# Giving out norm scalings two per step and moving three left-hand sums to other steps, in attention followed by a SwiGLU block

## The chip, the cores and the metric

The kernel runs on one core of a Trainium2 chip. A core has five engines that matter here, each with its own queue of instructions in program order: TensorE (PE, matmuls, with its weight loads shown as PEld), VectorE (DVE), ScalarE (ACT), GpSimd (POOL), and SyncE (SP), which issues the DMAs. The metric is the device time of one execution in microseconds (us); less is better. All arithmetic is in fp32.

## The reference: what is computed

Attention over 8 sequences, 12 heads, 448 positions and 64 dimensions a head, with queries and keys normalised by their root mean square, then a feed-forward block on the same rows.

```python
q_n, k_n = rmsnorm(q, g_q), rmsnorm(k, g_k)
attn = softmax(q_n @ k_n.T / sqrt(64))          # per sequence and head
x = (attn @ v)                                  # (8, 12, 448, 64) -> (3584, 768)
xn = x / sqrt(mean(x * x) + 1e-6) * rms_g
out = (silu(xn @ w_gate) * (xn @ w_val)) @ w_out   # 768 -> 1536 -> 768
```

## The kernel before

**Tiling and stages.** A loop runs over 48 pairs of heads (six to a sequence). The attention of a pair takes four PE steps of score and value matmuls. Between the pairs lie the feed-forward items of earlier sequences, some to each slot. When sequence s is through attention, its rows x are normalised by `norm_x` (L732). Then come the output products of sequence s-1, and after them the gate and value products of sequence s. The gate and value products (L1182) use a fast scheme of 15 block products for 3 by 3 blocks. The left operands that this scheme needs are sums of blocks of x, made on DVE by L772.

**The output product.** For sequences 2, 3, 5, 6 and 7 there are four tiles of 128 rows (some carried over from the sequence before), and `out_quads` (L1462) multiplies them with `w_out` by two nested levels of a seven-product scheme in Strassen's manner. The outer level has seven products, i = 0 to 6. The outer left sums are made by L1364. Inside each outer product i stand seven inner products, whose left operands are A11, A12, A22 and the four inner sums S1 = A21 + A22, S2 = S1 - A11, S3 = A11 - A21 (which is written over A21), S4 = A12 - S2. All inner sums are made on DVE by `left_q1` (L1384), so they all stand in the trace under L1392, and all are 128x384. An inner product is three matmuls in the program and six in the trace (an fp32 matmul shows as two records).

An outer product is done in four PE steps. Step `a` (12 records) uses A11 and A12, `bb` (12) S2 and then S3, `c` (12) A22 and then S1, `d` (6) S4. The order is a(0), bb(0), c(0), a(1), d(0), bb(1), c(1), a(2), d(1), and so on: **d(i) comes after a(i+1), and bb(i+1) comes right after d(i)**. At the very end c(6) is followed by d(6): in sequence 7 directly, in the others with one gate product between.

**What DVE does in each step.** After a(i), L1538 adds the two halves of a PSUM bank. After bb(i), L1543 and L1544 add into a running tile. After c(i), L1552 adds that tile to the bank of c. The matmuls of d(i) go into half of that same bank, so they can't begin before L1552 has read it. After d(i), L1564 adds the last piece, and `finish(i)` has POOL add whole tiles (L1489). Before the change, the sums are put there as follows, behind the adds of the same step in DVE's queue:

- bb(i): S4 of i, then S1 of i+1 (for i = 1, S1 comes in c instead)
- c(i): S2 and S3 of i+1 (for i = 1: first all outer sums still waiting, by `hurry`, then S1, S2, S3)
- d(i): none

Other DVE work falls between these steps: after each one, either one waiting outer sum (L1364) or one sum of x (L772) is issued, and DVE's reductions for the query and key norms (L496) come too.

**norm_x.** It puts a transposed 1/rms into a PSUM bank `rb` (from the four banks that the attention scores also rotate through), and six DVE instructions (L744, 128x448, for hp = 0 to 5) scale the six parts of x with it. The bank comes free after the sixth. For sequences 2 to 7, scaling hp is put behind the step hp steps later; for sequence 1 they go three per step, for sequence 0 all at once.

**What sets the order.** Nothing is planned by cost: `pe(fn)` counts one step, emits its instructions, and then those that `after(n, fn)` put off to this step. Every engine runs its queue in exactly that order.

Of the kernel before, what the change touches and what calls it, by code (L numbers as in the profile page):

```python
# [335 lines left out]
def safe_scores(  # L336
# [42 lines left out]
    def after(n, fn):  # L379
        due.append((now["t"] + n, fn))  # L380
# [351 lines left out]
    def norm_x(b):  # L732


        rs = st.pop(("rx", b))
        ps = (ps_s if b else ps_f).tile([128, 512], F32, name="rb", tag="s" if b else "f")
        for t in range(NT):
            nc.tensor.transpose(ps[:, t * P:(t + 1) * P], rs[:, t:t + 1].to_broadcast([P, 128]), ident[0:P, 0:P])

        whole = st["x", b]  # L740

        def scale(hp):
            x = whole[:, hp, :]
            nc.vector.scalar_tensor_tensor(x, x, rg[:, hp:hp + 1], ps[:, 0:S], ALU.mult, ALU.mult)  # L744

        for hp in range(NPAIR):
            if b:
                after(hp // 3 if b == 1 else hp, lambda hp=hp: scale(hp))
            else:
                scale(hp)  # L750
        if b == 0:
            return

        parts = st.pop(("x", b)).rearrange("p (h c) n -> p h c n", h=2)
        a = st["left", b] = {f"a{i + 1}{k + 1}": parts[:, :, k, i * HT:(i + 1) * HT] for i in range(2) for k in range(3)}

        def place(name):
            if name in OVER:
                return a[OVER[name]]
            if name in MADE[:4]:  # L760
                t = s_pool.tile([128, S], F32, name="xs")
            elif name in ("S2", "S0"):
                t = l2_pool.tile([128, S], F32, name="l2")
            else:
                t = more_x[("S4", "S5", "S13").index(name)]
            return t.rearrange("p (h n) -> p h n", h=2)

        def op(name):
            first, second, what = LEFT_G[name]
            one, two = a[first], a[second]  # L770
            a[name] = place(name)
            nc.vector.tensor_tensor(a[name], one, two, what)  # L772

        slow.extend((name, lambda name=name: op(name)) for name in MADE)
        st["x_at"] = now["t"]
# [46 lines left out]
    ORDER_Q = ("B11", "B21", "T2", "T3", "T4", "T1", "B22")  # L822
# [64 lines left out]
    def data(key):  # L887
        return st[key][0][:, 0:GW if key[0] == "wg" else BW]
# [99 lines left out]
    def out_pairs(b):  # L988
        return (((0, 1),), ((-1, 0), (1, 2)), ((-1, 0), (1, 2)), ((0, 1), (2, 3)))[b % 4]
# [394 lines left out]
    def left_q1(b, i, which):  # L1384

        of = lambda name: left_q(b, i, name)
        for at in which:
            to, first, second, what = (("S1", "A21", "A22", ALU.add), ("S2", "S1", "A11", ALU.subtract),
                                       ("S3", "A11", "A21", ALU.subtract), ("S4", "A12", "S2", ALU.subtract))[at]
            if to != "S3":  # L1390
                st["l2", b, i, to] = l2_pool.tile([128, S], F32, name="l2")[:, 0:KG * 128].rearrange("p (c n) -> p c n", c=KG)
            nc.vector.tensor_tensor(of(to), of(first), of(second), what)  # L1392
# [69 lines left out]
    def out_quads(b):  # L1462

        bank, dst, steps = {}, {}, []
        tiles = [i for pair in out_pairs(b) for i in pair]
        left = {}
        for key in stream_q(b):
            left[key] = min(2, PARTS_Q - 2 * key[3])

        def rows(name):  # L1470

            if name in ("B11", "T1"):
                tag = "pa"
            elif name in ("T2", "T3"):
                tag = {"T2": "pb", "T3": "pc"}[name]
            else:
                tag = None
            if tag:
                t = tmp.tile([128, 2, S], F32, name=tag, tag=tag, bufs=1)
                return [t[:, row, 0:BW] for row in range(2)]  # L1480
            return [y_pool.tile([128, HALF], F32, name="y", tag="y") for _ in range(2)]

        def out(what, n, first):
            for row in range(2):
                after(4, lambda row=row: store(b, n, tiles[first + row], what[row]))

        def add(to, one, other):
            for row in range(2):
                nc.gpsimd.tensor_tensor(to[row], one[row], other[row], ALU.add)  # L1489

        def finish(i):
            name, m = ORDER_Q[i], dst[i]
            if name == "B21":
                add(m, m, dst[0])
                out(m, 0, 0)
            elif name == "T2":
                add(m, m, dst[0])
            elif name == "T3":
                add(m, m, dst[2])
            elif name == "T4":  # L1500
                add(m, m, dst[3])
                out(m, 0, 2)
            elif name == "T1":
                add(dst[3], dst[3], m)
                add(m, m, dst[2])
                out(dst[3], 1, 2)
            elif name == "B22":
                for row in range(2):
                    nc.vector.tensor_tensor(m[row], m[row], dst[5][row], ALU.add)
                out(m, 1, 0)  # L1510

        def term(i, at, ps, start=True):

            a = left_q(b, i, ("A11", "A12", "S2", "S3", "A22", "S1", "S4")[at])
            for j in range(KG):
                n = at * KG + j
                key = ("wq", b, i, n // 2)
                nc.tensor.matmul(ps, lhsT=a[:, j, :], rhs=data(key)[:, n % 2 * HW:(n % 2 + 1) * HW], start=start and j == 0,  # L1518
                                 stop=j == KG - 1, skip_group_check=True)
                left[key] -= 1  # L1520
                if not left[key]:
                    used(key)

        def two(i, what):
            ps = bank[i, what] = ps_f.tile([128, 512], F32, name="ff", tag="f")[:, 0:BW].rearrange("p (h n) -> p h n", h=2)
            for h in range(2):
                term(i, 2 * "abc".index(what) + h, ps[:, h], start=h == 0)
            return ps

        def lo_hi(tile):  # L1530
            return tile[:, 0:HW], tile[:, HW:BW]

        def a(i):
            ps = two(i, "a")
            dst[i] = rows(ORDER_Q[i])
            q1 = st["q1", b, i] = tmp.tile([128, S], F32, name="th", tag="th", bufs=2)[:, 0:HW]
            nc.scalar.copy(q1, ps[:, 0])
            nc.vector.tensor_tensor(lo_hi(dst[i][0])[0], ps[:, 1], q1, ALU.add)  # L1538

        def bb(i):  # L1540
            ps = two(i, "b")
            u = st["u", b, i] = tmp.tile([128, S], F32, name="th", tag="th", bufs=2)[:, 0:BW].rearrange("p (h n) -> p h n", h=2)
            nc.vector.tensor_tensor(u[:, 0], ps[:, 0], st.pop(("q1", b, i)), ALU.add)  # L1543
            nc.vector.tensor_tensor(u[:, 1], ps[:, 1], u[:, 0], ALU.add)  # L1544
            left_q1(b, i, (3,))
            if i == 0 or i > 1 and i + 1 < len(ORDER_Q):
                left_q1(b, i + 1, (0,))

        def c(i):
            ps = two(i, "c")  # L1550
            u3 = st["u", b, i][:, 1:2].to_broadcast([128, 2, HW])
            nc.vector.tensor_tensor(dst[i][1].rearrange("p (h n) -> p h n", h=2), ps, u3, ALU.add)  # L1552
            if i == 1:
                hurry(first_sums)
                left_q1(b, i + 1, (0,))
            if i + 1 < len(ORDER_Q):
                left_q1(b, i + 1, (1, 2))
            if i + 2 == len(ORDER_Q):
                st["l2 done", b] = True

        def d(i):
            ps = bank[i, "c"]
            term(i, 6, ps[:, 1], start=False)
            nc.vector.tensor_tensor(lo_hi(dst[i][0])[1], ps[:, 1], st.pop(("u", b, i))[:, 0], ALU.add)  # L1564
            finish(i)

        full = 2 * KG * HW
        if b == B - 1:
            steps.append((0, idle))
        for i in range(len(ORDER_Q) + 1):  # L1570
            if i < len(ORDER_Q):
                steps.append((full, lambda i=i: a(i)))
            if i:
                steps.append((full // 2, lambda i=i - 1: d(i)))
            if i < len(ORDER_Q):
                steps += [(full, lambda i=i: bb(i)), (full, lambda i=i: c(i))]
        return steps
# [185 lines left out]
    scale = norm_rests(0, 0, 2)  # L1763
# [12 lines left out]
    for g in range(NG + 1):  # L1776
        b, hp = divmod(g, NPAIR)
# [138 lines left out]
```

## Time and profile before

| what | us |
|---|---|
| median of 3 runs (1531.54 to 1534.40) | 1532.55 |
| the execution that was profiled | 1533.21 |
| span of its instructions in the profile | 1531.4 |
| PE busy in that span | 1484.1 |
| DVE busy | 1039.9 |
| POOL busy | 738.6 |
| ACT busy | 604.0 |

The profiled execution is 1.8 us longer than its span, which is what lies around the first and last instruction. It is 0.66 us above the median. In the lines of the profile, "x<-a,b" names the tile written and the tiles read, L is the line of the kernel, and a bracket at the end gives the idle time of the engine before the instruction and what ended it. Times of the trace are counted from the start of the span. The output products of sequence 2 begin at 616.0, of sequence 3 at 804.7, of sequence 6 at 1330.8 and of sequence 7 at 1471.6. Sequence 5's repeat those of sequence 3 some 344 us later.

### The profile page before, as it was taken

The numbers are of one execution on the slowest core, as the hardware profiler recorded it, in microseconds if no ns is written. First come the engines' busy times: TensorE is split into PE (matmuls) and PEld (weight loads), VectorE is DVE, ScalarE is ACT, GpSimd is POOL, SyncE is SP. The second block draws the span as 40 slices with busy tenths as digits, with TensorE's granted clock in tenths as the row PEclk, the third lists the DMA queues.
The fourth block names the chain that finished last, engine by engine and source line by source line (L and its number), as shares of the span: only waits on it lengthen the run. The fifth ranks groups of instructions, "written<-read, shape, count | busy, mean of one in ns | idle before, by whom it ended". The sixth has DMA issues, their size and how long they took to land.

```text
span 1531.4 us, 25718 instructions
## 1 busy us (share of the span) xinstructions
PE 1484.1 (97%) x8732; PEld 1155.8 (75%) x8732; DVE 1039.9 (68%) x1826; ACT 604.0 (39%) x1377; POOL 738.6 (48%) x708
## 2 busy tenths in 40 slices
PE   8999999998999999899999999999999999999997
PEld 4344445687755888787988788759788789899996
DVE  5777999687855687874568655635668655674664
ACT  6856765344322443224442443334542443201100
POOL 6967987555433453364544644345644632021002
PEclk9999999999999999999999999999999999999998
DMA  7758675775577899885557865576457755597675
GB/s 190 224 164 237 183 237 169 231 250 187 188 235 231 283 309 317 285 254 191 174 152 237 247 186 160 162 228 190 133 162 246 223 157 145 154 301 227 167 237 170
DMA packets 302176, 322.51 MB, mean 211 GB/s; under 512 B 81620, under 2 KB 243668, under 8 KB 302036
## 3 DMA queue, kind: packets, MB, share of 16 engines
q1 hardware_dynamic: 301108, 320.58, 68.8%
q8 instruction: 72, 1.18, 0.3%
q14 instruction: 68, 0.56, 0.1%
q10 hardware_dynamic: 800, 0.20, 0.1%
q0 software_dynamic: 128, 0.00, 0.0%
HBM read 266.90 MB, written 53.77 MB: 209 GB/s over the span
## 4 chain that ended last, share of the span: by engine, by line
PE 83%; DVE 10%; DMA 2%; issue 2%; SPq 1%; ACT 1%; POOL 1%; DVEq 0%; POOLq 0%; ACTq 0%
PE ff L1182 37%; PE ff L1518 12%; PE sc L659 8%; PE av L674 7%; PE ff L1589 6%; PE ff L1447 5%; PE tr L545 2%; PE ff L1320 1%; PE den L692 1%; DVE l L1392 1%; PE den L607 1%; PE sc L563 1%; DMA vt<-in_v_dram 1%; PE av L590 1%; DVE ms L496 1%
## 5 line engine op out<-in xcount | busy, mean ns | idle before, releaser
L714 POOL TENSOR_TENSOR es<-es,e 128x448 f32<-128x448 f32 x205 | 252.2, 1230 | 13.6
L1182 PE MATMUL ff<-x,w 128*128 128x224 f32 x1272 | 254.0, 353 | 1.4 <-DVE pb L1203 1.1
L1182 PEld LDWEIGHTS ff<-x,w 128*128 128x128 f32 x1272 | 238.5, 190 | 4.2 <-DVE pb L1203 1.4
L659 PE MATMUL sc<-qT,kT 64*64 64x448 f32 x1176 | 232.7, 541 | 5.6 <-DVE x L744 3.9
L674 PE MATMUL av<-e,vt 64*64 64x448 f32 x984 | 193.3, 538 | 0.0
L664 ACT ACTIVATE e<-sc 128x448 f32<-128x448 f32 x294 | 155.0, 547 | 80.9 <-PE sc L659 59.4
L1182 PE MATMUL ff<-xs,w 128*128 128x224 f32 x848 | 168.4, 353 | 2.6 <-DVE w L1087 1.3
L1182 PEld LDWEIGHTS ff<-xs,w 128*128 128x128 f32 x848 | 158.6, 190 | 6.3 <-issue 3.4
L644 POOL TENSOR_TENSOR ss<-ss,rd 128x448 f32<-128x448 f32 x40 | 46.8, 1170 | 210.3 <-ACT rd L643 210.3
L659 PEld LDWEIGHTS sc<-qT,kT 64*64 64x64 f32 x1176 | 78.8, 133 | 88.2 <-issue 59.9
L709 POOL TENSOR_TENSOR es<-e 128x448 f32<-128x448 f32 x41 | 47.3, 1154 | 192.5 <-ACT e L664 192.5
L1518 PE MATMUL ff<-w,l 128*128 128x192 f32 x630 | 119.1, 331 | 6.8 <-DVE pb L1552 3.0
L1203 DVE TENSOR_TENSOR pc<-ff,l 128x448 f32<-128x448 f32 x56 | 34.9, 623 | 122.9 <-PE ff L1182 91.7
L515 POOL TENSOR_TENSOR rs<-ms,mhalf 128x12 f32<-128x12 f32 (+1 forms) x50 | 115.3, 2307 | 4.2
L1518 PEld LDWEIGHTS ff<-w,l 128*128 128x128 f32 x630 | 104.2, 191 | 13.8 <-DVE pb L1552 4.2
L1589 PE MATMUL ff<-x,w 128*128 128x448 f32 x288 | 111.8, 541 | 0.0
L674 PEld LDWEIGHTS av<-e,vt 64*64 64x64 f32 x984 | 66.0, 133 | 41.3 <-issue 41.3
L1200 DVE TENSOR_TENSOR pb<-ff,pb 128x448 f32<-128x448 f32 x84 | 52.4, 623 | 63.0 <-PE ff L1182 53.5
L1589 PEld LDWEIGHTS ff<-x,w 128*128 128x128 f32 x288 | 53.3, 190 | 51.1 <-issue 47.6
L1182 PE MATMUL ff<-top_x,w 128*128 128x224 f32 x424 | 89.4, 361 | 2.1 <-DVE w L1090 2.1
L1182 PEld LDWEIGHTS ff<-top_x,w 128*128 128x128 f32 x424 | 80.2, 193 | 13.4 <-issue 10.2
L1489 POOL TENSOR_TENSOR y<-y,pa 128x384 f32<-128x384 f32 x10 | 11.3, 1154 | 157.4 <-DVE y L1564 144.4
(210 smaller groups left out, 2892.2 us busy)
## 6 DMA issues: line engine op xcount, KB each, us to landing
w<-kept SPq DMA_DIRECT2D x383, 256.0 KB, 3.4
w<-kept_q SPq DMA_DIRECT2D x350, 192.0 KB, 3.8
w<-kept_o SPq DMA_DIRECT2D x150, 192.0 KB, 4.0
kept_q<-w SPq DMA_DIRECT2D x63, 192.0 KB, 3.4
qk<-in_q_dram SPq DMA_DIRECT2D x48, 192.0 KB, 3.8
qk<-in_k_dram SPq DMA_DIRECT2D x96, 96.0 KB, 3.8
raw<-in_moe_w_gate_dram SPq DMA_DIRECT2D x24, 384.0 KB, 4.5
raw<-in_moe_w_val_dram SPq DMA_DIRECT2D x24, 384.0 KB, 4.3
```

The source lines that it names most:

```text
L515: nc.gpsimd.tensor_tensor(st["rs", g][:, cols], ms, mhalf[:, cols], ALU.pow)
L644: after(m, lambda: (nc.gpsimd.tensor_tensor(ss, ss, rd, ALU.add), st.update({("summed", b): hp})))
L659: nc.tensor.matmul(ps[r, 0:S], lhsT=st["kT", g][r, keys_of(i)], rhs=st["qT", g][r, :], start=True, stop=True)
L664: nc.scalar.activation(e, ps[:, 0:S], ACT.Exp)
L674: nc.tensor.matmul(st["av", g][own(j), 0:S], lhsT=vt, rhs=st["e", g, i][r], start=i == 0, stop=i == PARTS - 1, skip_group_check=True)
L709: nc.gpsimd.tensor_tensor(st["es", g], st["e", g, 0], st["e", g, 1], ALU.add)
L714: nc.gpsimd.tensor_tensor(st["es", g], st["es", g], st["e", g, i], ALU.add)
L1182: nc.tensor.matmul(bank[:, w * HT:(w + 1) * HT], lhsT=data(key)[:, (2 * w + c) * 128:(2 * w + c + 1) * 128], rhs=a[left][:, c, :], start=o ...
L1200: nc.vector.tensor_tensor(T[name], ps[:, 0:S], T[name], ALU.add)
L1447: nc.tensor.matmul(ps, lhsT=left_o(b, which, LEFT_O[name], c), rhs=data(("wo", b, name, c)), start=first and c == 0, stop=c == NFP - 1, sk ...
L1518: nc.tensor.matmul(ps, lhsT=a[:, j, :], rhs=data(key)[:, n % 2 * HW:(n % 2 + 1) * HW], start=start and j == 0, stop=j == KG - 1, skip_grou ...
L1589: nc.tensor.matmul(bank[w][:, 0:S], lhsT=data(key)[:, c * 128:(c + 1) * 128], rhs=st["x", 0][:, 3 * half + c, :], start=half == c == 0, st ...
```

## The change

The scalings of `norm_x` for sequences 2 to 7 go two per step (steps 0, 0, 1, 1, 2, 2) instead of one (0 to 5). Of the inner sums, S4 of i moves from bb(i) to c(i), where it stands behind L1552 and ahead of everything else; S3 of i+1 moves from c(i) to d(i), behind L1564; S2 of i+1 stays in c(i), and now follows S4. No instruction is added or taken away, and no PE step moves.

```diff
         for hp in range(NPAIR):
             if b:
-                after(hp // 3 if b == 1 else hp, lambda hp=hp: scale(hp))
+                after(hp // (3 if b == 1 else 2), lambda hp=hp: scale(hp))
...
         def bb(i):
...
             nc.vector.tensor_tensor(u[:, 1], ps[:, 1], u[:, 0], ALU.add)
-            left_q1(b, i, (3,))
             if i == 0 or i > 1 and i + 1 < len(ORDER_Q):
                 left_q1(b, i + 1, (0,))
...
         def c(i):
...
             nc.vector.tensor_tensor(dst[i][1].rearrange("p (h n) -> p h n", h=2), ps, u3, ALU.add)
+            left_q1(b, i, (3,))
             if i == 1:
                 hurry(first_sums)
                 left_q1(b, i + 1, (0,))
             if i + 1 < len(ORDER_Q):
-                left_q1(b, i + 1, (1, 2))
+                left_q1(b, i + 1, (1,))
...
         def d(i):
...
             finish(i)
+            if i + 1 < len(ORDER_Q):
+                left_q1(b, i + 1, (2,))
```

In `left_q1` the numbers 0, 1, 2, 3 stand for S1, S2, S3, S4.

## The prediction

> **What bounds the kernel now.** I read the page first (busy shares), then the table of waits of TensorE, then the timeline of TensorE, VectorE and GpSimd through the output products of sequences 2, 3, 6 and 7.
>
> ```profile
> span 1531.4 us, 25718 instructions
> PE 1484.1 (97%) x8732; PEld 1155.8 (75%) x8732; DVE 1039.9 (68%) x1826; ACT 604.0 (39%) x1377; POOL 738.6 (48%) x708
> ```
>
> TensorE is busy for 97% of the span, so 1531.4 - 1484.1 = 47.3 us of idle time is all that a change of order can win. The waits of TensorE say which of it the moved instructions touch:
>
> ```profile
> PE sc L659 <- DVE x L744: 3.9, 1, 3.9
> PE ff L1518 <- DVE pb L1552: 3.0, 3, 1.0
> ...
> PE ff L1518 <- DVE pa L1552: 1.8, 4, 0.5
> ...
> PE ff L1518 <- DVE l L1392: 1.3, 2, 1.1
> ...
> PE ff L1518 <- DVE raw L1392: 0.5, 3, 0.2
> ```
>
> One score matmul waits for the last scaling (L744), since it takes over the bank rb. Steps d wait for L1552, steps bb for S2 (tile l) and S3 (raw). In these stretches VectorE is the late one: the end of sequence 3's output shows it without a gap.
>
> ```profile
> 861.24 0.54 DVE L1552 TENSOR_TENSOR pa<-ff,th 128x384 f32<-128x384 f32 x1
> 861.70 1.31 DVE L1392 TENSOR_TENSOR l<-l,raw 128x384 f32<-128x384 f32 x1
> 862.93 1.48 DVE L1392 TENSOR_TENSOR raw<-raw 128x384 f32<-128x384 f32 x1
> 864.34 0.61 DVE L772 TENSOR_TENSOR l<-x,top_x 128x448 f32<-128x448 f32 x1
> 864.87 0.34 DVE L1538 TENSOR_TENSOR y<-ff,th 128x192 f32<-128x192 f32 x1
> 865.14 0.61 DVE L772 TENSOR_TENSOR l<-x,top_x 128x448 f32<-128x448 f32 x1
> 865.67 0.34 DVE L1564 TENSOR_TENSOR pa<-ff,th 128x192 f32<-128x192 f32 x1
> ```
> ```profile
> 861.83 2.47 PE L1518 MATMUL ff<-w,l 128*128 128x192 f32 x12 [0.51 <-DVE pa L1552]
> 864.47 2.22 PE L1518 MATMUL ff<-w,raw 128*128 128x192 f32 x12 [0.16 <-DVE raw L1392]
> ```
> ```profile
> 858.52 5.48 POOL L714 TENSOR_TENSOR es<-es,e 128x448 f32<-128x448 f32 x4
> ```
>
> S2(6) and S3(6) take 1.31 and 1.48 instead of 0.55 us beside four GpSimd adds. S3(6) ends at 864.41, and TensorE goes on with bb(6)'s second half at 864.47. Where VectorE isn't behind, as in sequence 7, the rhythm is this:
>
> ```profile
> 1493.48 2.11 PE L1518 MATMUL ff<-w,l 128*128 128x192 f32 x12
> 1495.43 1.79 PE L1518 MATMUL ff<-w,h 128*128 128x192 f32 x10
> ```
> ```profile
> 1494.66 0.36 DVE L1564 TENSOR_TENSOR pb<-ff,th 128x192 f32<-128x192 f32 x1 [0.22 <-PE ff L1518]
> ```
>
> The first 12 records are d(2) and bb(3)'s S2 half, 0.975 us each. bb(3) begins at 1494.46, its S3 half at 1495.43, and L1564 starts 0.20 us after bb(3) began.
>
> [...] the sums measured alone take 0.55 us, and 1.3 to 1.5 us where L714 or L1489 runs; L1552, which has one input in PSUM, stays at 0.54. [...] After the 3.86 us gap the granted clock from 632 to 637 was 0.66, and score matmuls took 1.01 instead of 0.54 us.
>
> **Prices.** A VectorE instruction lets the next start after 0.27 us (128x192), 0.47 (a sum), 0.54 (L772) or 0.59 (L744); these are start-to-start distances. TensorE restarts 0.055 us after the end of the sum it waited for (1348.054 to 1348.109), and its next record then comes 0.267 instead of 0.163 us later. A wait therefore costs the end of the sum + 0.16 - the planned start.
>
> **Part 1, the scalings.** They are the same instructions, earlier. In sequence 2 the sixth started at 631.73, behind four sums L1150 to L1153 that GpSimd's adds stretched to 1.3 us; now it goes by 624. From the start of that attention block to bb(1)'s second half sequence 2 took 636.98 - 623.87 = 13.11 us, sequence 3, without the wait, 820.13 - 812.56 = 7.57. So 5.5 us can be won. Next late there is S3(1), see part 2. In the other sequences no wait on L744 over 0.1 us goes away. Against this, three steps carry 1.2 us more of VectorE each. In sequences 2 and 3 an attention block follows and hides it. In sequence 6 none follows: there VectorE is already late, L1552(0) starts at 1338.33 and d(0) starts 0.21 us late. Of the queue from 1331.32 on, the scalings hp 2 to 5 now stand ahead of L1552(0), where only hp 2 stood; S4(0) left. So L1552 moves by 3 x 0.59 - 0.47 = 1.3 to 1339.64, S4(0), now behind it, ends at 1340.66, and d(0), planned for 1338.57, is held for 2.25 instead of 0.47 us: **+1.8 us**.
>
> **Part 2, the sums.** Three things happen.
>
> *S3 comes just too late everywhere.* It now waits for d(i)'s matmuls and L1564. Counted from bb(i+1)'s start: L1564 at 0.20, S3 from 0.47 to 1.02, TensorE at 1.075; the S3 half was planned at 0.975. Cost 1.02 + 0.16 - 0.975 = 0.2 us for every clean transition. I count 2 clean ones each in sequences 2, 3, 5 and 6, and 4 in sequence 7. Only a turn of queries or keys between d and bb (0.33 to 0.43 us) hides it. In d(0) of sequences 3 and 5 a GpSimd add is running (the sum at 819.63 took 0.73): 0.4 us. [...] I take 0.2, because S3 starts before L1489.
>
> *S2(2) moves back by one sum in c(1)*, behind S4(1): it ended at 826.28, now 826.75, and bb(2) was due at 826.41: +0.5 us in sequences 2, 3, 5 and 7.
>
> *Where VectorE is behind, S3 now queues behind everything of steps c, a and d.* At i = 5 of sequence 3, S3(6) ended at 864.41. The four instructions that followed it, L772, L1538, L772, L1564, now stand ahead of it: 0.54 + 0.27 + 0.54 + 0.27 = 1.6 us, up to 2.0 with the lock at L772. bb(6)'s second half goes from 864.47 to 866.1 to 866.5; I take **+1.8 us** (range 1.0 to 2.2) for each of sequences 2, 3 and 5, with every wait before it absorbed. At i = 2, L1552(2) does come some 1.5 us earlier (S4(2) left its front, 0.66, and one lock), but d(2) needs S4(2), which is now 0.47 or, locked, 1.1 us behind L1552. Ends of S4(2) between 832.9 and 834.3 by who gets the lock, against a planned 832.3 to 832.8: the old wait of 1.26 becomes 0.8 to 1.7. I take no change. S3(3) then ends 0.27 us late.
>
> Sums by sequence. Sequence 3 (and 5): 0.4 + 0.5 + 0 + 0.3 + 0.2 + 1.8 (the second clean one is within the 1.8) + 0.1 for d(6) = 3.3 each. Sequence 2: after the attention block VectorE is busy with L1150 to L1153 until 631.8, so L1564(0) starts at 632.1, S3(1) ends at 632.9, and bb(1)'s second half goes from 636.98 to 632.96: -4.0, then + 0.5 + 0.3 + 0.2 + 1.8 + 0.1 = -1.1. Sequence 6: +1.8 for d(0); +0.5 for S3(1) behind L1538, an outer sum and L1564; -0.4 for S2(2), since VectorE catches up during the wait; +1.1 for S3(2) behind two L772; -0.4 for d(2); +0.4, +0.2, +0.2, +0.4 for S3(3) to S3(6); +0.2 for d(6): +4.0. Sequence 7: 0.4 + 0.5 + 4 x 0.2, and at the end d(6), which waits for L1552 anyway (0.71 us), now also for S4(6), which ends at 1520.06: +0.4, together +2.1. The S4 of the other steps has 1.95 us of a(i+1) as cover and needs 1.2; without a(i+1) it would cost what it costs at the end.
>
> Total: 3.3 + 3.3 - 1.1 + 4.0 + 2.1 = **+11.6 us** on the profiled 1533.21; on the median of the runs 1532.55 + 11.6 = 1544.2.
>
> **Rivals.** (a) *The wait sums are partly absorbed*: only the firm terms hold (12 clean S3 at 0.2 = 2.4, S2(2) 2.0, half of the i = 5 terms 2.7, half of sequence 6's d(0) 0.9, tail 0.4, less 4.0 in sequence 2): +4.4, 1537. For it: a stall gives VectorE time to catch up. Against it: S3's chain starts at TensorE itself. (b) *Gain and loss cancel*, within 0.2% (about 3 us, what a measurement here can tell from no change): 1532.5. It needs i = 5 to cost nothing. (c) *Faster*: the lightened bb decides. If S3 is in time, that is, if L1564 and S3 together take under 0.92 us after bb's start (I find 1.02) and VectorE has no queue at d, then all listed waits go: 5.5 in sequence 2, 2.7 in each of 2, 3 and 5 (1.26 at d(2), 1.46 from d(5) on), 2.2 in 6, 0.5 in 7 = 16.3; less the tail 0.4: 1516.6. For it: L1552 is the commonest releaser, and it does move forward. Against it: d then waits for S4 behind L1552, and the timeline above has a queue at d(5).
>
> **How the numbers follow.** Forecast (+7 to +18) 0.60, (a) 0.20, (b) 0.08, (c) 0.12. Slower 0.80, same 0.08, faster 0.12. Own range of the forecast: 1540 to 1550. With (a) and the edge of (b) the range is 1533 to 1550, leaving out (c) and the tails.
>
> **What would show it.** Right: weight loads of L1518 wait for `h L1392` and `raw L1392` at nearly every bb, and matmuls over 1 us at bb(6) of sequences 2, 3 and 5 (a clean wait of 0.1 us leaves no gap on the matmul row, whose records overlap by 0.16; it shows in their starts); `x L744` is gone; L1552 gives way to `l L1392` (S4) at d(2). The step d to bb's second half in sequence 7 goes from 1.95 to 2.15 us. Wrong: waits on L1392 no more than before, or bb(6) with no wait. The whole is wrong if the stretches of sequences 2 to 7 come out shorter.

## The result and the profile after

The changed kernel takes 1547.26 us (median of 6 runs, 1546.62 to 1549.11), against 1533.47 us for the kernel before in the same comparison: a ratio of 1.0091, 95% interval 1.0072 to 1.0111. It is slower by 13.8 us. The forecast was 1544.2, that is +11.6.

The page of the profile after, engines and span:

```profile
span 1544.8 us, 25720 instructions
PE 1489.5 (96%) x8732; PEld 1154.2 (75%) x8732; DVE 1044.1 (68%) x1826; ACT 603.9 (39%) x1377; POOL 742.9 (48%) x708
```

The span grew by 13.4 us. TensorE's idle time grew from 47.3 to 55.3 us, and its busy time by 5.4: the first record after a wait is itself longer (0.43 instead of 0.33 us), and the first 0.16 us of a wait lie under the record before it, where they count as busy. The work is the same, so order alone cost this. The table of TensorE's waits in the profile after (total us, times, longest):

```profile
PE ff L1518 <- DVE l L1392: 9.8, 17, 2.0
PE ff L1518 <- DVE raw L1392: 6.3, 5, 1.8
...
PE ff L1518 <- DVE h L1392: 3.2, 5, 1.3
```

The waits on L744 and on the add behind c (L1552, now L1551) have left the table. In their place stand 19.3 us of waits on inner sums: on `l`, which is S4 (and S2), and on `raw` and `h`, which is S3. Before, sums held TensorE for 1.8 us in all.

For each sequence I compared the stretch from the first to the last matmul of its output product. Times are us, relative to the kernel before:

| stretch of sequence | forecast | measured |
|---|---|---|
| 2 | -1.1 | -0.9 |
| 3 | +3.3 | +4.3 |
| 5 | +3.3 | +4.1 |
| 6 | +4.0 | +4.2 |
| 7 | +2.1 | +2.15 |
| sum | +11.6 | +13.9 |

These five stretches hold the whole loss; outside them the span shrank by 0.5 us. The clean rhythm of sequence 7, which the prediction showed for before, TensorE first, then VectorE:

```profile
1505.52 2.11 PE L1518 MATMUL ff<-w,l 128*128 128x192 f32 x12
1507.57 2.22 PE L1518 MATMUL ff<-w,h 128*128 128x192 f32 x12
```
```profile
1506.69 0.36 DVE L1564 TENSOR_TENSOR pb<-ff,th 128x192 f32<-128x192 f32 x1 [0.22 <-PE ff L1518]
1506.97 0.55 DVE L1392 TENSOR_TENSOR h<-h 128x384 f32<-128x384 f32 x1
```

d(2) to bb(3)'s second half now takes 2.05 us instead of 1.95, and the half itself 0.1 longer. S3 ends at 1507.52, TensorE starts at 1507.57. No idle time shows on the matmul row, since records overlap. The loss of 0.2 us shows only in the starts.

The end of sequence 3's output, which stood before the change at 861.24 to 865.67. VectorE, TensorE and GpSimd of the profile after:

```profile
861.16 1.31 DVE L1392 TENSOR_TENSOR l<-raw,l 128x384 f32<-128x384 f32 x1
862.40 1.48 DVE L1392 TENSOR_TENSOR l<-l,raw 128x384 f32<-128x384 f32 x1
863.80 1.55 DVE L772 TENSOR_TENSOR l<-x,top_x 128x448 f32<-128x448 f32 x1
865.28 0.34 DVE L1538 TENSOR_TENSOR y<-ff,th 128x192 f32<-128x192 f32 x1
865.54 0.61 DVE L772 TENSOR_TENSOR l<-x,top_x 128x448 f32<-128x448 f32 x1
866.08 0.34 DVE L1564 TENSOR_TENSOR pa<-ff,th 128x192 f32<-128x192 f32 x1
866.35 0.54 DVE L1392 TENSOR_TENSOR raw<-raw 128x384 f32<-128x384 f32 x1
```
```profile
862.53 1.24 PE L1518 MATMUL ff<-w,l 128*128 128x192 f32 x6 [0.37 <-DVE l L1392]
863.93 1.24 PE L1518 MATMUL ff<-w,l 128*128 128x192 f32 x6 [0.16 <-DVE l L1392]
866.94 2.22 PE L1518 MATMUL ff<-w,raw 128*128 128x192 f32 x12 [1.76 <-DVE raw L1392]
```
```profile
859.40 5.47 POOL L714 TENSOR_TENSOR es<-es,e 128x448 f32<-128x448 f32 x4
```

The rows are S4(5), S2(6), a sum of x, the add behind a(6), a sum of x, the add behind d(5), and only then S3(6). TensorE waits for that last row, 1.76 us. d(5) and the first half of bb(6) wait a little, as they did before, but d(5) now for S4(5) and no longer for the add of c.

### The profile page after: what moved, and what is told of

Its sections match the earlier page's. It is cut to its first block, busy times and chain, and to the rows that moved or that the text cites. A ratio compares the mean times of both kernels' runs of the same rounds, so it can differ in the third digit from the quotient of the medians.

```text
span 1544.8 us, 25720 instructions
## 1 busy us (share of the span) xinstructions
PE 1489.5 (96%) x8732; PEld 1154.2 (75%) x8732; DVE 1044.1 (68%) x1826; ACT 603.9 (39%) x1377; POOL 742.9 (48%) x708
## 4 chain that ended last, share of the span: by engine, by line
PE 80%; DVE 13%; DMA 2%; issue 1%; ACT 1%; POOL 1%; SPq 0%; DVEq 0%; POOLq 0%; ACTq 0%
PE ff L1182 37%; PE ff L1518 11%; PE sc L659 7%; PE av L674 7%; PE ff L1447 5%; PE ff L1591 5%; DVE l L1392 2%; PE tr L545 2%; PE ff L1320 2%; PE den L692 1%; PE sc L563 1%; PE den L607 1%; PE av L590 1%; DVE ms L496 1%; DVE xs L772 1%
## 5 line engine op out<-in xcount | busy, mean ns | idle before, releaser
L714 POOL TENSOR_TENSOR es<-es,e 128x448 f32<-128x448 f32 x205 | 251.2, 1225 | 13.6
L644 POOL TENSOR_TENSOR ss<-ss,rd 128x448 f32<-128x448 f32 x40 | 46.7, 1168 | 209.8 <-ACT rd L643 209.8
L709 POOL TENSOR_TENSOR es<-e 128x448 f32<-128x448 f32 x41 | 48.3, 1178 | 199.4 <-ACT e L664 199.4
L1518 PE MATMUL ff<-w,l 128*128 128x192 f32 x630 | 118.8, 330 | 10.3 <-DVE l L1392 9.8
L1518 PEld LDWEIGHTS ff<-w,l 128*128 128x128 f32 x630 | 103.3, 190 | 18.3 <-DVE l L1392 16.2
L1489 POOL TENSOR_TENSOR y<-y,pa 128x384 f32<-128x384 f32 x10 | 12.5, 1272 | 156.1 <-DMA w<-kept_q 115.0
```

The lines of the kernel that those rows point to most:

```text
L644: after(m, lambda: (nc.gpsimd.tensor_tensor(ss, ss, rd, ALU.add), st.update({("summed", b): hp})))
L709: nc.gpsimd.tensor_tensor(st["es", g], st["e", g, 0], st["e", g, 1], ALU.add)
L714: nc.gpsimd.tensor_tensor(st["es", g], st["es", g], st["e", g, i], ALU.add)
```

## The experiments

Theory A is that of the prediction: S3 behind L1564 is the cost, S4 behind L1552 takes over the old wait, and the scalings win in the stretch of sequence 2 and lose in that of 6. Theory B blames the crowded scalings, theory C the S4 behind L1552. "Stretches" below are sums over the five stretches, against the kernel before.

**The scalings alone.** The kernel before with the first hunk of the change only:

```diff
-                after(hp // 3 if b == 1 else hp, lambda hp=hp: scale(hp))
+                after(hp // (3 if b == 1 else 2), lambda hp=hp: scale(hp))
```

> Only the scalings two per step; all inner sums as before the change. Theory A (S3 put behind L1564 makes the loss, the scalings win in sequence 2 and lose in sequence 6): bb(1)'s second half of sequence 2 comes 5.5 us earlier, d(0) of sequence 6 1.8 us later, of which S2(2) gives back up to 0.9; nothing else moves; total -3.5 to -4.5 us against before. Theory B (the crowded scalings make the loss): slower than before by over 5 us. Theory C (S4 behind L1552 makes the loss): as A.

Measured: 1529.92 us, ratio 0.9968 (0.9953 to 0.9984), stretches -3.3. Sequence 2 won 5.6, sequence 6 lost 2.55, 3, 5 and 7 moved by 0.1 or less. So the scalings are a gain, and theory B falls. In sequence 6 d(0) came 1.8 later, and then another 1.7 was lost up to c(1), of which bb(2) gave 0.9 back. No wait stands there. The TensorE row shows why, with the granted clock of the same stretch below (window, length, busy times, PEclk, DMA):

```profile
1336.88 3.27 PE L1518 MATMUL ff<-w,l 128*128 128x192 f32 x12 [2.00 <-DVE pa L1552]
```
```profile
1336.00:1342.00 6.00, 5.12 (x21) 5.12 (x22) 3.90 (x10) 0.00 (x0) 0.00 (x0) 0.72 0.61 186
```

Behind the 2.0 us wait the 12 records took 3.27 us instead of 2.22, at a granted clock of 0.72. The expectation had no such term; the last section says in which runs it came.

**The sums alone.** The change without its first hunk.

> Only the inner sums moved; the scalings one per step as before. Theory A: +17 us against before (sequence 2 +3.4, 3 and 5 +4.2 each, 6 about +3, 7 +2.1), that is more than the whole change. Theory B: within 3 us of before. Theory C: as A. The wait of the scores on L744 (3.9 us) is back.

Measured (one execution): 1548.57 us, stretches +13.05 (sequence 2 -1.1, 3 and 5 +4.2 each, 6 +3.6, 7 +2.15). The sums carry the loss, as expected, but the 17 was wrong: of the 3.9 us wait on L744 in sequence 2 only 0.6 came back. Two more waits on L744, 0.6 us each, are new in the stretches of sequences 3 and 5; they cost 0.75 each there, while S3(1) cost only 0.2. VectorE in sequence 2 of that run:

```profile
628.44 0.36 DVE L1150 TENSOR_TENSOR w<-w 128x192 f32<-128x192 f32 x1
...
629.37 1.18 DVE L1153 TENSOR_TENSOR w<-w 128x192 f32<-128x192 f32 x1
630.47 0.67 DVE L744 SCALAR_TENSOR_TENSOR x<-x,rg,rb 128x448 f32<-128x448 f32 x1
```

With S3(1) gone from the burst, three of the four sums L1150 to L1153 passed while GpSimd's add L709 ran from 628.20 to 630.33 (0.36 us each; before the change three of the four took 1.3). The sixth scaling followed 3 us sooner by that. The two hunks therefore don't add up: the scalings win 5.6 us in that stretch beside the old sums, and there the moved sums had already freed most of it.

**S3 in d, but ahead of L1564.** From the changed kernel, the same step and one place further forward:

```diff
             term(i, 6, ps[:, 1], start=False)
+            if i + 1 < len(ORDER_Q):
+                left_q1(b, i + 1, (2,))
             nc.vector.tensor_tensor(lo_hi(dst[i][0])[1], ps[:, 1], st.pop(("u", b, i))[:, 0], ALU.add)
             finish(i)
-            if i + 1 < len(ORDER_Q):
-                left_q1(b, i + 1, (2,))
```

> The changed kernel, with S3 of i+1 still issued in step d(i), but ahead of that step's add L1564, so that it waits for no matmul of d. Theory A: the clean waits of 0.2 us go to 0 (sequence 7 from +2.15 to about +0.95), S3(1) of sequences 3 and 5 (1.17 each) goes to 0, S3(6) of sequences 2, 3 and 5 stays at 1.3 of 1.6 since its queue (two L772 and L1538) stays ahead of it; total about +7.5 against before instead of +13.5. Theory B and C: no change from the changed kernel (+13.5).

Measured (one execution): 1539.06 us, stretches +6.1. Sequence 7 fell from 2.15 to 1.03, all of its clean waits were gone. S3(1) of sequences 3 and 5 cost nothing, S3(6) 1.35. So 13.9 - 6.1 = 7.8 us of the loss hang on S3 standing behind an add that waits for d's matmuls.

**S3 back in c.** The changed kernel with S3 behind S2 in c(i); S4 stays behind L1552.

```diff
             if i + 1 < len(ORDER_Q):
-                left_q1(b, i + 1, (1,))
+                left_q1(b, i + 1, (1, 2))
...
             finish(i)
-            if i + 1 < len(ORDER_Q):
-                left_q1(b, i + 1, (2,))
```

> The changed kernel, with S3 of i+1 back in c(i) behind S2; S4 stays in c(i) behind L1552, scalings stay two per step. Theory A: S3 waits vanish; left are S2(2) (+0.5 in sequences 2, 3, 5, 7), d(0) of sequence 6 (+1.8), the end of sequence 7 (+0.46), d(6) (+0.3 each), less 5.5 in sequence 2: about +0.5 against before (-2 to +2). Theory B: stays over +5. Theory C: stays at +10 or more, since S4 still lies behind L1552.

Measured (one execution): 1534.81 us, stretches -0.1. Theory C falls as the account of the loss: with S4 still behind L1552, sequences 3 and 5 lose 0.3 each (S2(2) costs 0.47, d(2) gives that back, and d(3) costs 0.3), sequence 7 0.93 (S2(2) and its end) and sequence 6 3.6 (after a 1.99 us wait 12 records took 3.31 us, at a granted clock of 0.66 from 1337 to 1342), against -5.2 in sequence 2. S3's place in d costs 13.9 + 0.1 = 14 us, as much as the whole loss. Here the clock slowed in sequence 6, which it did not in the changed kernel (1.00 from 1346 to 1352), so 14 is, if anything, too small. S4's move isn't free either. This run and that of the scalings alone differ in S4's place and in nothing else, so beside the new scalings it costs 3.1 us (from -3.25 to -0.11), about what the scalings win.

**S3 one step earlier, in a.** The changed kernel with S3(i) behind L1538 of a(i).

```diff
             nc.vector.tensor_tensor(lo_hi(dst[i][0])[0], ps[:, 1], q1, ALU.add)
+            if i:
+                left_q1(b, i, (2,))
...
             finish(i)
-            if i + 1 < len(ORDER_Q):
-                left_q1(b, i + 1, (2,))
```

> The changed kernel, with S3 of i put in step a(i) (behind L1538 of a(i), ahead of d(i-1)) instead of d(i-1): one step earlier than the change has it, and ahead of the sum of x that follows a. Theory A (what costs is S3 standing behind a step that ends just before it is needed): clean waits 0, S3(1) of sequences 3 and 5 at 0, S3(6) of sequences 2, 3 and 5 late by 0.54 (L772) + 0.27 (L1538) = 0.8 plus at most one lock instead of 1.60; total +3 to +5 against before. If only the number of sums in a step mattered (a, bb, c and d hold 1, 1, 2 and 0 here, against 0, 1, 2 and 1), it would stay at +13.5.

Measured (one execution): 1536.79 us, stretches +0.95, better than expected. Clean waits and S3(1) were gone, and S3(6) was late by 0.80, the figure that the queue gave. The miss is in sequence 6, which lost 1.3 instead of the 4.2 of the changed kernel: the waits for S3(2) and S3(1) behind sums of x and outer sums went too.

**No sums of x ahead of S3(6).** The changed kernel, with the sums of x held back behind c(5) and a(6).

```diff
         def a(i):
             ps = two(i, "a")
+            if i == 6:
+                st["no_sum"] = now["t"]
...
         def c(i):
             ps = two(i, "c")
+            if i == 5:
+                st["no_sum"] = now["t"]
...
-            elif slow and now["t"] - st["block"] > 4 and now["t"] - st["x_at"] >= NPAIR and may_make(slow[0][0]):
+            elif slow and now["t"] != st.get("no_sum") and now["t"] - st["block"] > 4 and now["t"] - st["x_at"] >= NPAIR and may_make(slow[0][0]):
```

> The changed kernel, but no sum of x (L772) is issued behind c(5) and a(6); they follow two steps later. Theory A (S3(6) is late because two L772 and L1538 stand ahead of it): bb(6)'s second half in sequences 2, 3 and 5 comes 1.1 to 1.5 us earlier, its +1.60 falls to 0.1 to 0.5; d(6) may lose up to 0.5 of it; sequence 6's S3(6) loses its wait beyond 0.2; all else as in the changed kernel: total about -3 to -4 us against the changed kernel. If the lock with the GpSimd adds alone makes S3(6) late, it stays at +1.2 or more.

Measured (one execution): 1540.32 us, stretches +7.7. VectorE at the end of sequence 3:

```profile
858.79 1.48 DVE L1392 TENSOR_TENSOR l<-l,raw 128x384 f32<-128x384 f32 x1
860.19 0.35 DVE L1540 TENSOR_TENSOR y<-ff,th 128x192 f32<-128x192 f32 x1
860.46 0.34 DVE L1568 TENSOR_TENSOR pa<-ff,th 128x192 f32<-128x192 f32 x1
860.72 0.96 DVE L1392 TENSOR_TENSOR raw<-raw 128x384 f32<-128x384 f32 x1
```

S3(6) follows S2(6) after two short adds, and in none of the three sequences does bb(6)'s second half fall further behind: the 1.60 is gone, 4.8 us in all. That is more than expected, and so is the whole gain of 6.2 us against the changed kernel. The other 1.4 us come mostly from S3(1) of sequence 3, which here was not held by a GpSimd add and took 0.55 us. So the queue ahead made S3(6) late (in which one sum of x was itself held by an add, 1.55 us), not an add beside S3(6), which itself took 0.96 us here.

**Scalings two per step for the x of sequence 3 alone**, in the kernel before:

```diff
-                after(hp // 3 if b == 1 else hp, lambda hp=hp: scale(hp))
+                after(hp // (3 if b == 1 else 2 if b == 3 else 1), lambda hp=hp: scale(hp))
```

> The kernel before, with the scalings two per step only for the x of sequence 3 (the one whose bank held the scores up, in the stretch of the output of sequence 2); all sums as before. Theory A: that stretch -5.6 us as in the run of the scalings alone, sequence 6's +2.55 gone, nothing else moves: -5.6 us, ratio 0.9963. If the win came from all sequences together it would be smaller.

Measured: 1527.99 us, ratio 0.9959 (0.9947 to 0.9972), stretches -5.3, all in sequence 2. The gain is one wait in one place, with the slow clock behind it (0.50 from 632.3 to 635.7 in the kernel before).

**The same, and the sums of x held back behind bb(2).**

```diff
         def bb(i):
             ps = two(i, "b")
+            if i == 2:
+                st["no_sum"] = now["t"]
```

(with the condition on `no_sum` as above)

> The kernel before, with the scalings two per step for the x of sequence 3 alone, and no sum of x (L772) behind bb(2), so that L1552(2) no longer stands behind one that waits for a GpSimd add. Theory A: -5.6 as in the run without the second edit, and the wait of d(2), 1.26 us in each of sequences 2, 3 and 5 and 0.4 in 6, goes: another -3.5 to -4.2; total -9 to -10 us, ratio 0.994. If the late sum of x then holds up what follows it, the second edit is worth nothing.

Measured: 1525.46 us, ratio 0.9956 (0.9940 to 0.9972), stretches -6.8 instead of the expected -9 to -10. d(2) came 1.16 us earlier, but d(3) gave 0.64 back: the late sum of x now fell behind bb(3), ahead of L1552(3), and waited there for GpSimd's L1489.

**The same, held back behind bb(2) and bb(3)** (`i in (2, 3)`).

> As the run with the scalings of sequence 3 alone and no sum of x behind bb(2), but none behind bb(3) either. There d(2) won 1.2 us and d(3) gave back 0.64 + 0.10, because the late sum of x fell behind bb(3) and waited there for GpSimd's L1489. Theory A (a sum of x between S1 and L1552 is what holds d up): d(2) keeps its 1.2 us in sequences 2, 3 and 5 and d(3) gives nothing back; total -9 us against before, ratio about 0.994. If the give-back only moves on to d(4) or bb(4), it stays at -7.

Measured: 1524.69 us, ratio 0.9936 (0.9921 to 0.9951), stretches -8.9, which is the lowest median here, ahead of both kernels. Its interval overlaps that of the run before, so only the stretches tell these two apart. The kernel before at d(2) of sequence 3, VectorE and TensorE:

```profile
829.96 1.48 DVE L1392 TENSOR_TENSOR l<-h,h 128x384 f32<-128x384 f32 x1
831.37 1.55 DVE L772 TENSOR_TENSOR xs<-x 128x448 f32<-128x448 f32 x1
832.84 0.55 DVE L1552 TENSOR_TENSOR pb<-ff,th 128x384 f32<-128x384 f32 x1
```
```profile
833.44 1.24 PE L1518 MATMUL ff<-w,l 128*128 128x192 f32 x6 [1.00 <-DVE pb L1552]
```

The same place in this run:

```profile
824.21 1.48 DVE L1392 TENSOR_TENSOR l<-h,h 128x384 f32<-128x384 f32 x1
825.62 0.54 DVE L1554 TENSOR_TENSOR pb<-ff,th 128x384 f32<-128x384 f32 x1
```
```profile
824.58 2.11 PE L1518 MATMUL ff<-w,h 128*128 128x192 f32 x12
826.52 1.14 PE L1518 MATMUL ff<-w,l 128*128 128x192 f32 x6
```

L1552(2) (here L1554) follows S1 directly, and d(2) starts 1.94 us after a(3), with no wait. S4 is still in bb(2) here. So the sum of x between S1 and L1552 is enough to explain the wait of d(2).

## Why the prediction was right

**The prices** held. TensorE restarted 0.05 us after the sum it waited for, and its next record came 0.1 us late, so a clean transition cost 0.20 (0.10 at the start of the half and 0.10 behind it), as in the sum. There are four in sequence 7, two each in 3, 5, 2 and 6. Weight loads of L1518 waited on L1392 46 times instead of 8, as named.

**The bound** of 47.3 us was not put to the test by a loss, and it isn't strict: here order alone moved the busy time by 5.4 us. Three more readings of the prediction are off without harm to its sum. The three steps carry 0.6 us more of scalings each, not 1.2 (the 3 x 0.59 that it used is right). Of the four sums L1150 to L1153 only three were stretched to 1.3 us. And the sign it named for sequence 7, from 1.95 to 2.15 us, came as 2.05, since half of the 0.2 falls behind the start of the half.

**The scalings.** In sequence 2 bb(1) came 5.63 us earlier (forecast 5.5), and S3(1) then held its second half, as named: -4.2 us there, against a forecast -4.0. In sequence 6 d(0) came 1.78 later (forecast 1.8). The run of the scalings alone shows the same 1.78 without any S4 behind L1552, so there it is the scalings that decide, not S4. The wait in the changed kernel:

```profile
1347.67 2.22 PE L1518 MATMUL ff<-w,l 128*128 128x192 f32 x12 [1.99 <-DVE l L1392]
```

**S2(2)** cost 0.47 (forecast 0.5). **S3(6)** cost 1.60 (forecast 1.8), and with the two small shifts of d(5) and bb(6) ahead of it, 1.64. **The end** cost 0.46 (forecast 0.4).

**d(2)** lost and won nothing, as forecast, but by two errors that cancel. L1552(2) was to come some 1.5 us earlier. Counted from the start of a(3) it came 0.5 earlier, since the sum of x ahead of it took 1.55 us as before, beside a GpSimd add; S4 behind it was not held and took 0.47 again. In the profile after:

```profile
831.01 1.55 DVE L772 TENSOR_TENSOR xs<-x 128x448 f32<-128x448 f32 x1
832.49 0.55 DVE L1551 TENSOR_TENSOR pb<-ff,th 128x384 f32<-128x384 f32 x1
832.96 0.54 DVE L1392 TENSOR_TENSOR l<-raw,l 128x384 f32<-128x384 f32 x1
```

**The term that was too small** is "In d(0) of sequences 3 and 5 a GpSimd add is running (the sum at 819.63 took 0.73): 0.4 us." It measured 1.17 and 0.92. In the profile after, the row of S3(1), the wait it caused, and GpSimd's adds are these:

```profile
818.10 1.51 DVE L1392 TENSOR_TENSOR h<-h 128x384 f32<-128x384 f32 x1
```
```profile
819.66 2.22 PE L1518 MATMUL ff<-w,h 128*128 128x192 f32 x12 [0.91 <-DVE h L1392]
```
```profile
813.51 1.86 POOL L709 TENSOR_TENSOR es<-e 128x448 f32<-128x448 f32 x1 [9.82 <-ACT e L664]
815.45 3.75 POOL L714 TENSOR_TENSOR es<-es,e 128x448 f32<-128x448 f32 x3
```

S3 waited for a whole add instead of the rest of one: the last of the three adds began 0.03 us before it. I took the duration from a sum that had met the end of an add. But the first add, L709, here took 1.86 us instead of 1.15, and those behind it came later by that. In the run without sums of x ahead of S3(6), whose VectorE queue is the same through this stretch up to S3(1), the same S3(1) started 0.01 us behind the add, took 0.55 us and cost 0.2; there the add took 1.55. So where GpSimd's adds stand at that moment decides, to within hundredths of a microsecond. That term should have stood as 0.2 to 1.2. It makes 1.3 of the 2.3 us by which the forecast fell short. The rest is a balance of small terms: the second clean transition of sequences 3 and 5, which I had put inside the 1.8 (0.2 each), d(6), which cost 0.4 instead of 0.1 there, and 0.2 each in sequences 2 and 6, less 0.16 for S3(6) and 0.09 at d(0) in each of 3 and 5.

**The rivals.** (a), with the long waits half absorbed, was too kind: the stalls of TensorE gave S3(6) no lead, and it cost 1.60 instead of 0.9. (b) needed that term to be nothing. (c) failed at the point that was named: L1564 and S3 end 1.02 us after bb's start and are needed after 0.975.

**What was luck.** Besides d(2), the clock of sequence 6. The prediction has no term for a clock that falls behind the longer wait at d(0). In the changed kernel it stayed at 1.00, and sequence 6 lost 4.2 us as forecast; in two other runs with the same wait it fell (0.72 and 0.66 over the stretch behind it), and in the run of the scalings alone that cost 1.7 us before bb(2) gave 0.9 back.

What stays open: what the S4 move costs with the old scalings and S3 in c was not tried by itself.

## What to carry to other kernels

When a stretch is late on one engine, moving an instruction to a less busy step helps only if its own result is still ready when it is due: count from the event that releases the new place to the moment the operand is due, and include all that the queue issues in between. Undo the parts of a mixed change one by one: here one hunk alone won 3.3 us in the stretches and the other alone lost 13.0, and one line of the winning hunk for a single sequence won more (5.3). Look for what stands directly ahead of the late instruction; it was a sum of another stage, and holding that back by a step or two won 3.6 us more.

## What the runs showed of the hardware

The TensorE clock dropped after waits shorter than the 3.86 us one of the kernel before, but not after each of them. Four runs show it at d(0) of sequence 6, behind a wait of 1.99 or 2.00 us:

| run | 12 records behind the wait | granted clock |
|---|---|---|
| the scalings alone | 3.27 us | 0.72 (1336 to 1342) |
| S3 back in c | 3.31 us | 0.66 (1337 to 1342) |
| the changed kernel | 2.22 us | 1.00 (1346 to 1352) |
| S3 in a | 2.22 us | 1.00 (1340 to 1346) |

S3 back in c and then the changed kernel, in the profile (window, length, busy time of PE first, PEclk third from the end):

```profile
1337.00:1342.00 5.00, 4.41 (x17) 4.41 (x18) 3.41 (x9) 0.00 (x0) 0.00 (x0) 0.66 0.64 203
```
```profile
1346.00:1352.00 6.00, 4.14 (x24) 3.85 (x25) 5.10 (x13) 0.09 (x1) 0.00 (x0) 1.00 0.70 221
```

What makes the difference between these runs was not shown, so whether the clock falls behind such a wait could not be forecast here.

Of the lock between VectorE and GpSimd that the prediction counts with, the profiles of the kernel before and of the changed one show this: 214 of their 280 inner sums (L1392) took 0.54 to 0.56 us. The other 66 took 0.58 to 1.51. Each of these began while a GpSimd instruction of L714, L1489, L644 or L520 ran, and ended 0.41 to 0.42 us after the end of it. It was seen the other way round too: in the run of the sums alone one GpSimd add L709 took 2.13 us, where its median in these two profiles is 1.14, with L1150 to L1152 passing while it ran.
